# Decay attention with a mixture of experts: fixed key/query tiles with constant rows, decay rows on 64 partitions, weights in nine transfers

## The chip, the cores and the metric

The kernel runs on one NeuronCore of a Trainium2 chip, and the time is the device time of one execution in microseconds, as a median of several. A NeuronCore has a matrix engine (TensorE, in the profile PE, with its weight loads as PEld), a vector engine (VectorE, DVE), an activation engine (ScalarE, ACT), a general engine (GpSimd, POOL) and a queue engine (SyncE, SP), which issues the transfers (DMAs). Each engine works through its own instructions in order and waits on semaphores for the others.

## The reference

Eight batches of eight heads, 576 positions, head width 64. First a causal attention with decay, then a mixture of four experts, each with an attention of its own on the result, of which the gate takes two per row:

```python
scores = scale * q @ k.T                       # (8, 8, 576, 576)
cum = cumsum(log(clip(f, 1e-4, 1)))
attn = softmax(causal(scores + cum[i] - cum[j]))
x = concat_heads(attn @ v)                     # (8, 576, 512)
for e in range(4):                             # experts
    qe, ke, ve = x @ wq[e], x @ wk[e], x @ wv[e]
    ye = softmax(causal(scale * qe @ ke.T)) @ ve @ wo[e]
    out += gate_top2(x @ w_gate)[e] * ye
```

## The kernel before

**Pairs.** The unit of work is a pair: two heads of a batch ("a", 32 of them) or two experts ("m", 16). The first eight pairs, those of batches 0 and 1, are all attention; from then on four attention pairs and two expert pairs alternate. For a pair the kernel does these tasks, each a Python generator:

- `prep_attn` loads keys and queries (`kn`, `qn`, two transfers each), transposes them on PE (`tp`), copies the rounded part to the tile `kq` (ACT, L229), and the difference to `ka` (DVE, L230), eight of each per pair; two transfers copy `kq` rows to `ka`. `prep_moe` does the same with projections (`pp`).
- `max_pass` multiplies queries by keys (PE, L378, tile `m`) and takes the maximum of each row (DVE, L384, L395, L422, L428). The maxima are transposed, negated (ACT, L435, `ms`), and two transfers (L199, called in line 439) write them to row 68 of `kq`.
- `scores` makes two products for each block: L464 with `ka`, and L465 with `kq`, which carries the decay and the maximum. ACT takes the exponential (L481, L491, L496, L508), POOL sets the upper triangle to zero and adds up the rows (`R`).
- `attend` multiplies by the values (PE, L551, tiles `oa` and `ob`); `row_sums` and `apply_rows` divide; `moe_front` and `project_out` are the experts' gate, values and output.

**Decay.** `kq` holds 64 rows of keys and queries and five rows more: the product of the rows 64 to 68 adds decay, minus decay and minus the maximum. So the products take 68 and 69 rows (`K = 68`, `K = 69`). `decay_rows` works the decay out on 32 partitions (one pair of heads each, two halves of 576), then writes a table `ex` of 33 entries in DRAM, three transfers of ones and minus ones and two of the decay. `extra_rows` gives pair 0 and 1 (`DIRECT = 2`) their rows directly (two memsets on POOL, two transfers), and every later pair by one transfer of 5 rows from `ex`; an expert pair takes entry 32, whose decay is zero. The tiles `kq`, three of them, are taken in turn from a pool.

**Weights.** `load_weights` brings four matrices and the gate in 18 transfers through staging tiles; ACT rounds them (L175), POOL makes the remainder (L176).

**What sets the order.** Each task has a start and an end in units of pairs (`PLAN`, `HEAD`, `TAIL`, `W`), and a heap in the last lines of the function takes the generators' steps by their due time. So the tables write the order of the program; the tile framework then moves instructions on an engine a little by its own estimate. On the chip each engine keeps the order that results. `load_weights` is due from -1.0 to 0.2, that is before the first pair's scores.

## Time and profile before

| | |
|---|---|
| three runs, median (lowest, highest) | 796.29 us (794.36, 798.07) |
| the profiled execution | 794.9 us, of it the span 793.2 us |
| busy PE, PEld, DVE, ACT, POOL | 740.0, 600.7, 581.6, 472.8, 400.8 us |
| share of the span | 93%, 76%, 73%, 60%, 51% |
| moved by the DMA engines | 73.3 MB, 92 GB/s on average |

The span runs from the first to the last instruction of one execution. A busy share is an average over stages with different limits: a stage in which DVE or a transfer is waited for doesn't show in the 93% of PE. The rows below are therefore taken by stretch.

### The profile page before, as it was taken

The page shows a single profiled execution, that of the slowest core. Times are in us where ns is not written, and L with a number is a line of the kernel's source. Part 1 is how long each engine was busy: PE and PEld are TensorE (multiplying, and loading weights), DVE is VectorE, ACT ScalarE, POOL GpSimd, SP SyncE. Part 2 cuts the span into 40 slices and gives each one's busy share as a digit, 9 for nine tenths or more (in the row PEclk, how much of TensorE's full clock was granted, in tenths as well). Part 3 has the DMA queues.
Part 4 walks back from the last instruction along what each step waited for, and adds up shares of the span by engine and source line. Part 5 has one row for each costly group of instructions (what it writes and reads, how often), then busy time and mean ns, then how long its engine had stood idle before and what let it go on. Part 6 is the DMA issues. An engine that isn't in the chain of part 4 may idle for free.

```text
span 793.2 us, 16781 instructions
## 1 busy us (share of the span) xinstructions
PE 740.0 (93%) x5704; PEld 600.7 (76%) x5704; DVE 581.6 (73%) x1858; ACT 472.8 (60%) x1152; POOL 400.8 (51%) x763
## 2 busy tenths in 40 slices
PE   3698999998999999999999999999999999989987
PEld 2475678776897788877887778878887768869854
DVE  7557786898777797787777787778777877764633
ACT  5465664575657674676556665667655755555443
POOL 7556472556446564547444644465544564473270
PEclk9998999999999999999999999999999999999999
DMA  7865541254424632355323542256323442203103
GB/s 187 194 138 118 98 105 32 58 123 89 91 51 105 145 86 49 84 128 139 79 63 87 127 107 63 52 135 147 78 65 79 112 102 57 55 21 70 58 14 106
DMA packets 143231, 73.32 MB, mean 92 GB/s; under 512 B 124085, under 2 KB 124565, under 8 KB 143081
## 3 DMA queue, kind: packets, MB, share of 16 engines
q1 hardware_dynamic: 143147, 72.26, 39.9%
q8 instruction: 45, 0.74, 0.4%
q14 instruction: 39, 0.32, 0.1%
HBM read 32.68 MB, written 10.96 MB: 55 GB/s over the span
## 4 chain that ended last, share of the span: by engine, by line
PE 74%; DVE 8%; ACT 6%; DMA 5%; SPq 3%; issue 2%; POOL 2%; POOLq 0%; ACTq 0%; DVEq 0%
PE pp_m L352 13%; PE ob_a L551 9%; PE pv L276 6%; PE po L678 6%; PE s_a L464 6%; PE s_a L465 6%; PE m_a L378 5%; PE tp_a L221 3%; PE ob_m L551 3%; PE m_m L378 3%; PE s_m L464 3%; PE s_m L465 3%; PE oa_a L551 2%; DVE junk_a L384 2%; PE sm_a L594 2%
## 5 line engine op out<-in xcount | busy, mean ns | idle before, releaser
L230 DVE TENSOR_TENSOR ka_a<-tp_a,kq_a 64x288 fp32r<-64x288 f32 x256 | 113.0, 451 | 25.0 <-ACT kq_a L229 19.4
L384 DVE CUSTOM_DVE_ANT_0 junk_a<-m_a,mask 128x192 bf16<-128x192 f32 (+2 forms) x192 | 93.3, 486 | 48.2 <-PE m_a L378 28.6
L464 PE MATMUL s_a<-ka_a 128*128 128x320 f32 (+4 forms) x384 | 115.8, 319 | 1.7 <-ACT P_a L481 1.1
L378 PE MATMUL m_a<-kq_a 68*128 68x320 f32 (+4 forms) x384 | 103.5, 337 | 14.0 <-DMA kq_a<-chl 7.8
L229 ACT ACTIVATE kq_a<-tp_a 64x288 fp32r<-64x288 f32 x256 | 99.1, 403 | 28.7 <-DVE ka_a L230 18.8
L465 PE MATMUL s_a<-kq_a 69*128 69x320 f32 (+4 forms) x384 | 104.8, 302 | 3.1 <-DMA kq_a<-ms_a 3.1
L450 POOL TENSOR_SCALAR_AFFINE_SELECT P_a<-P_a 128x128 f32<-128x128 f32 x128 | 37.5, 295 | 107.5 <-ACT P_a L496 96.1
L483 POOL TENSOR_SCALAR_AFFINE_SELECT P_a<-P_a 128x256 f32<-128x256 f32 x64 | 26.1, 408 | 125.8 <-ACT P_a L481 124.1
L378 PEld LDWEIGHTS m_a<-kq_a 68*128 68x128 f32 (+1 forms) x384 | 65.5, 191 | 26.4 <-issue 9.1
L359 ACT ACTIVATE kq_m<-pp_m 64x288 fp32r<-64x288 f32 x128 | 51.5, 405 | 51.4 <-PE pp_m L352 29.9
L360 DVE TENSOR_TENSOR ka_m<-pp_m,kq_m 64x288 fp32r<-64x288 f32 x128 | 57.8, 454 | 31.6 <-ACT kq_m L359 27.0
L464 PEld LDWEIGHTS s_a<-ka_a 128*128 128x128 f32 (+1 forms) x384 | 71.1, 186 | 8.8 <-ACT P_a L496 2.2
L519 POOL TENSOR_TENSOR R_a<-P_a 128x448 f32<-128x448 f32 x64 | 73.2, 1144 | 4.1
L551 PE MATMUL ob_a<-P_a,va 128*64 128x320 f32 (+1 forms) x512 | 73.8, 433 | 0.9 <-ACT ms_m L435 0.4
L465 PEld LDWEIGHTS s_a<-kq_a 69*128 69x128 f32 (+1 forms) x384 | 70.1, 186 | 5.7 <-DMA kq_a<-ms_a 4.3
L551 PEld LDWEIGHTS ob_a<-P_a,va 128*64 128x64 f32 x512 | 36.0, 144 | 33.4 <-issue 8.0
L464 PE MATMUL s_m<-ka_m 128*128 128x192 f32 (+3 forms) x192 | 57.9, 316 | 1.9 <-ACT P_m L496 1.2
L384 DVE CUSTOM_DVE_ANT_0 junk_m<-m_m,mask 128x192 bf16<-128x192 f32 (+2 forms) x96 | 46.6, 485 | 17.7 <-PE m_m L378 14.1
L520 POOL TENSOR_TENSOR R_a<-R_a,P_a 128x320 f32<-128x320 f32 x64 | 55.9, 875 | 1.1
L465 PE MATMUL s_m<-kq_m 69*128 69x192 f32 (+2 forms) x192 | 52.5, 300 | 3.3 <-DMA kq_m<-ms_m 3.2
L378 PE MATMUL m_m<-kq_m 68*128 68x192 f32 (+2 forms) x192 | 48.0, 317 | 0.6 <-DVE mxt_m L395 0.3
L276 PE MATMUL pv<-vh,xh_a 128*128 128x260 f32 x160 | 47.1, 294 | 1.1 <-DVE ka_a L230 1.0
(189 smaller groups left out, 2071.8 us busy)
## 6 DMA issues: line engine op xcount, KB each, us to landing
ka_a<-kq_a SPq DMA_DIRECT2D x64, 288.0 KB
kn_a<-in_k_dram SPq DMA_DIRECT2D x64, 144.0 KB
qn_a<-in_q_dram SPq DMA_DIRECT2D x64, 144.0 KB
ka_m<-kq_m SPq DMA_DIRECT2D x32, 288.0 KB
va<-in_v_dram SPq DMA_DIRECT2D x64, 128.0 KB
out_dram<-outb SPq DMA_DIRECT2D x32, 256.0 KB
kq_a<-ex SPq DMA_DIRECT2D x30, 45.0 KB
kq_a<-ms_a SPq DMA_DIRECT2D x64, 2.5 KB
```

Of the source, the lines that this page charges most:

```text
L229: nc.scalar.activation(hv, src, AF.Copy)
L230: nc.vector.tensor_tensor(lo[:, h, gs], src, hv.bitcast(F32), ALU.subtract)
L276: nc.tensor.matmul(pv[:, :NV], l[c][:, t0 : t0 + 128], r[:, c], start=(n == 0), stop=(n == 3 * KC - 1))
L352: nc.tensor.matmul(pp[:, :HS], w[:, c, es], x[c][:, gs], start=(n == 0), stop=(n == 3 * KC - 1))
L360: nc.vector.tensor_tensor(lo[:, h, gs], src, hv.bitcast(F32), ALU.subtract)
L378: nc.tensor.matmul(dst, qB[0:K, h, i0 : i0 + dst.shape[0]], kB[0:K, h, j0:j1], start=True, stop=True)
L384: nc.vector.tensor_tensor_reduce(jk[:, :n], src, mask[:, MW - n :], 1.0, init, ALU.add, ALU.max, acc)
L464: nc.tensor.matmul(dst, kaf[:, c : c + m], qA[:, h, i0:i1], start=True, stop=False)
L465: nc.tensor.matmul(dst, kqf[0:K, c + h * S : c + h * S + m], qB[0:K, h, i0:i1], start=False, stop=True)
L519: g.tensor_tensor(r[:, h, 128:S], q[:, 320:768], q[:, 768:1216], ALU.add)
L520: g.tensor_tensor(r[:, h, 256:S], r[:, h, 256:S], q[:, 1216:1536], ALU.add)
L551: mm = nc.tensor.matmul(dst[64 * h : 64 * h + 64, c0 : c0 + rhs.shape[-1]], vs[h][0:kp, blk], rhs, start=first, stop=last,)
```

## The change

- Four fixed tiles `kq0` to `kq3` take turns. `constant_rows` fills the rows 64 to 127 once: ones on the key side, zeros on the query side, minus ones in two rows. So products take 128 rows (`K = 128`), and only the decay rows are brought for each pair.
- `decay_rows` works on 64 partitions, one head each, in one piece. The table `ex` has only the two decay rows per head: one transfer of them and one of zeros, in a task of its own. `extra_rows` brings them in two transfers per pair; only pair 0 takes them directly (`DIRECT = 1`, four transfers).
- The weights come in 9 transfers instead of 18, due from pair 1 to pair 4.
- The other constants move into a task (`constants`); the pool of `kn` and `qn` has four buffers instead of three; `chl` lies in another pool; a scratch area for DMAs is smaller.

```diff
-    nat = ctx.enter_context(tc.tile_pool(name="nat", bufs=3))
+    nat = ctx.enter_context(tc.tile_pool(name="nat", bufs=4))
...
+    kqs = [const.tile([128, 2, 2, S], F32R, name=f"kq{i}") for i in range(NKQ)]
...
+    def constant_rows(kq, eng):
+        eng.memset(kq[64:128, :, 0].bitcast(F32), 1.0)
+        nc.gpsimd.memset(kq[64:128, :, 1].bitcast(F32), 0.0)
+        nc.gpsimd.memset(kq[64:66, :, 1].bitcast(F32), -1.0)
+
+    constant_rows(kqs[0], nc.vector)
...
-    DIRECT = 2
-    ex = dram.tile([NX, 2, 5, 2, S], F32, name="ex")
+    DIRECT = 1
+    ex = dram.tile([NP + 1, 2, 2, S], F32, name="ex")
...
     def decay_rows():
...
-        for h in range(2):
-            hs = slice(h * S, (h + 1) * S)
-            nc.vector.tensor_tensor_scan(cum[:, hs], pos1[:NP], lf[:, hs], 0.0, ALU.mult, ALU.add)
-            nc.scalar.activation(chl[:NP, 0, h], cum[:, hs], AF.Copy, scale=INV_SCALE)
...
-        for kq, r0, r1, src in ((0, 2, 5, pos1), (1, 0, 2, neg1), (1, 4, 5, pos1)):
-            nc.sync.dma_start(
-                ex[:, kq, r0:r1].rearrange("x r h s -> x (r h) s"),
-                src.unsqueeze(1).to_broadcast([NX, 2 * (r1 - r0), S]),
-            )
-        nc.sync.dma_start(ex[:, 0, 0:2], chl.bitcast(F32))
-        nc.sync.dma_start(ex[:, 1, 2:4], chl.bitcast(F32))
-        yield 0.5
+        nc.vector.tensor_scalar(ft, ft, 1.0e-4, 1.0, ALU.max, ALU.min)
+        nc.scalar.activation(lf, ft, AF.Ln)
+        nc.vector.tensor_tensor_scan(cum, pos1, lf, 0.0, ALU.mult, ALU.add)
+        nc.scalar.activation(chl[:, 0], cum, AF.Copy, scale=INV_SCALE)
+        nc.vector.scalar_tensor_tensor(
+            chl[:, 1], cum, INV_SCALE, chl[:, 0].bitcast(F32), ALU.mult, ALU.subtract
+        )
+        yield 1.0
+
+    def spread_rows():
+        nc.sync.dma_start(ex[:NP].rearrange("x h r s -> (x h) r s"), chl.bitcast(F32))
+        nc.sync.dma_start(
+            ex[NP].rearrange("h r s -> (h r s)").rearrange("(p c) -> p c", p=128), zero
+        )
+        yield 1.0
...
+                for e in range(0, E, 2):
+                    parts.append(
+                        (w[e : e + 2].rearrange("e (c p) d -> p (e c) d", p=128), 2, slice(D * e, D * e + 2 * D))
                     )
...
     def extra_rows(kq, x):
         if x < DIRECT:
-            nc.gpsimd.memset(kq[64:69].bitcast(F32), 1.0)
-            nc.gpsimd.memset(kq[64:66, :, 1].bitcast(F32), -1.0)
-            nc.sync.dma_start(kq[64:66, :, 0].bitcast(F32), chl[x : x + 1].bitcast(F32))
-            nc.sync.dma_start(kq[66:68, :, 1].bitcast(F32), chl[x : x + 1].bitcast(F32))
+            for h in range(2):
+                src = chl[2 * x + h : 2 * x + h + 1].bitcast(F32)
+                nc.sync.dma_start(kq[64:66, h, 0].bitcast(F32), src)
+                nc.sync.dma_start(kq[66:68, h, 1].bitcast(F32), src)
             return
-        nc.sync.dma_start(
-            kq[64:69].bitcast(F32), ex[x].rearrange("k r h s -> r h k s")
-        )
+        src = ex[x].rearrange("h r s -> r h s")
+        nc.sync.dma_start(kq[64:66, :, 0].bitcast(F32), src)
+        nc.sync.dma_start(kq[66:68, :, 1].bitcast(F32), src)
...
-        kB, qB, K = u["kB"], u["qB"], 68
+        kB, qB, K = u["kB"], u["qB"], 128
...
-        qA, qB, K = u["qA"], u["qB"], 69
+        qA, qB, K = u["qA"], u["qB"], 128
...
-    W = dict(d1=-0.8, l0=-1.0, l1=0.2)
+W = dict(d1=-1.9, l0=1.0, l1=4.0, c0=-1.7, c1=-1.3, x0=-0.9)
...
-    task(-1.99, W["d1"], 1.0, decay_rows)
+    task(-1.999, W["d1"], 1.0, decay_rows)
+    task(W["c0"], W["c1"], 1.0, constants)
+    task(W["x0"], W["x0"], 1.0, spread_rows)
     task(W["l0"], W["l1"], 4.0, load_weights)
```

The tables `PLAN`, `HEAD` and `TAIL` are the same in both. How the order changes is seen best on SP. Before, these rows of SP end with the two transfers that bring pair 0's maxima to its `kq` (`st` are staged weights, `ka_a_1` is pair 1, `x2` means twice in a row):

```order
L169 DMA st_k_319<-in_moe_wk_dram 128x4x64 x2
L199 DMA ka_a_1_254<-kq_a_1_255 64x2x576
L169 DMA st_k_333<-in_moe_wk_dram 128x4x64 x2
L169 DMA st_q_340<-in_moe_wq_dram 128x4x64 x2
L169 DMA st_q_353<-in_moe_wq_dram 128x4x64 x2
L199 DMA ka_a_1_254<-kq_a_1_255 64x2x576
L191 DMA kq_a_1_255<-chl 2x2x576
L192 DMA kq_a_1_255<-chl 2x2x576
L164 DMA st_o_365<-in_moe_wo_dram 128x512
L211 DMA kn_a_2_389<-in_k_dram 96x6x64 x2
L211 DMA qn_a_2_390<-in_q_dram 96x6x64 x2
L199 DMA kq_a_0_163<-ms_a_0_305 1x5x128 x2
```

Now the same place reads so (`kq_111`, `kq_112`, `kq_113` are the tiles of pairs 0, 1, 2):

```order
L244 DMA kn_a_3_476<-in_k_dram 96x6x64 x2
L244 DMA qn_a_3_477<-in_q_dram 96x6x64 x2
L282 DMA va_104<-in_v_dram 128x4x64
L231 DMA ka_a_2_345<-kq_113 64x2x576
L282 DMA va_104<-in_v_dram 128x4x64
L287 DMA va_104<-in_v_dram 64x2x64
L202 DMA st_v_504<-in_moe_wv_dram 128x8x64
L282 DMA va_105<-in_v_dram 128x4x64
L231 DMA ka_a_2_345<-kq_113 64x2x576
L282 DMA va_105<-in_v_dram 128x4x64
L287 DMA va_105<-in_v_dram 64x2x64
L231 DMA kq_111<-ms_a_0_295 1x5x128 x2
```

All weights but the first part have gone behind pair 0's maxima; keys and queries of pairs 2 and 3 and the values of pairs 0 and 1 have come ahead of them. On ACT the exponentials of pair 0 (`P_a_0`) now stand among the weights:

```order
L472 ACTIVATE ms_a_0_295<-mp_a_0_293 10x128
L205 ACTIVATE vh<-st_v_504 128x4x128
L521 ACT_TABLE_LOAD
L521 ACTIVATE P_a_0_327<-s_a_0_329 128x512
L205 ACTIVATE vh<-st_v_584 128x4x128
L205 ACTIVATE vh<-st_v_637 128x4x4
L521 ACTIVATE P_a_0_327<-s_a_0_377 128x512
L205 ACTIVATE kh<-st_k_698 128x4x128
L531 ACTIVATE P_a_0_327<-s_a_0_409 128x2x256
L472 ACTIVATE ms_a_1_417<-mp_a_1_415 10x128
L205 ACTIVATE kh<-st_k_766 128x4x128
```

Before, all eight conversions of weights (`vh`, `kh`, `qh`, `oh`, two each) stood ahead of the first exponential. On DVE, the difference for pair 2 (`ka_a_2`) stood among the maxima of pair 1, and now stands among those of pair 0 (`junk_a_0`):

```order
L263 TENSOR_TENSOR ka_a_2_345<-tp_a_2_352,kq_113 64x288
L126 CAST sel_100<-self_180 128x128
L421 ISA junk_a_0_253,mxs_a_0_233<-m_a_0_248,mask,mxt_a_0_235 128x256
L421 ISA mxs_a_0_233 128x1
L263 TENSOR_TENSOR ka_a_2_345<-tp_a_2_397,kq_113 64x288
L263 TENSOR_TENSOR ka_a_2_345<-tp_a_2_352,kq_113 64x288
L421 ISA junk_a_0_257,mxs_a_0_233<-m_a_0_255,mask 128x448
```

So DVE has a third pair's differences to make before the maxima of pair 0 are complete.

## Rows read from the trace of the kernel before

**Rows 1.** The page: span, and granted TensorE clock in 40 slices (tenths).

```profile
span 793.2 us, 16781 instructions
...
PEclk9998999999999999999999999999999999999999
```

**Rows 2.** Windows: busy us (count) per engine, granted clock, DMA share, GB/s.

```profile
0.00:20.00 20.00, 6.21 (x28) 4.63 (x28) 14.10 (x27) 10.37 (x22) 14.45 (x37) 1.00 0.77 186
20.00:39.40 19.40, 12.01 (x41) 8.84 (x40) 10.41 (x38) 8.06 (x14) 10.24 (x9) 1.00 0.88 195
39.40:50.00 10.60, 9.93 (x44) 8.07 (x46) 5.65 (x18) 8.00 (x22) 6.65 (x13) 1.00 0.77 164
50.00:110.00 60.00, 54.40 (x381) 38.48 (x382) 46.38 (x142) 34.89 (x88) 32.97 (x64) 0.91 0.52 108
...
200.00:700.00 500.00, 488.54 (x3925) 405.37 (x3923) 387.53 (x1269) 313.00 (x772) 254.36 (x489) 1.00 0.40 90
```

**Rows 3.** The chain that ended last, 0 to 40 us: start, length, what.

```profile
0.81 2.68 DMA fl<-in_f_dram
...
7.37 4.91 DMA kn_a<-in_k_dram
...
33.71 3.45 DMA st_o<-in_moe_wo_dram
```

**Rows 4.** Timeline, 18 to 45 us: start, length, engine, line, in brackets idle before.

```profile
18.93 1.30 PE L378 MATMUL m_a<-kq_a 68*128 68x192 f32 x4 [3.04 <-DMA kq_a<-chl]
...
31.19 1.30 PE L378 MATMUL m_a<-kq_a 68*128 68x192 f32 x4 [4.72 <-DMA kq_a<-chl]
...
32.06 1.55 SPq L199 DMA_DIRECT2D kq_a<-ms_a  x2
...
35.53 0.51 PE L465 MATMUL s_a<-kq_a 69*128 69x192 f32 x1
...
39.42 1.08 ACT L481 ACTIVATE P_a<-s_a 128x512 f32<-128x512 f32 x2
...
44.15 0.08 DVE L384 DVE_READ_ACCUMULATOR2_ANT mxs_a<- 128x1 f32 x1
```

**Rows 5.** Timeline, DVE: eight differences' rate, first and last of pair 0's maxima.

```profile
13.08 2.87 DVE L230 TENSOR_TENSOR ka_a<-tp_a,kq_a 64x288 fp32r<-64x288 f32 x6 [0.47 <-ACT kq_a L229]
...
19.78 0.36 DVE L384 CUSTOM_DVE_ANT_0 junk_a<-m_a,mask 128x192 bf16<-128x192 f32 x1 [2.04 <-PE m_a L378]
...
25.66 0.28 DVE L428 TENSOR_REDUCE mxs_a<-mx_a 64x2 f32<-64x128 f32 x1
```

**Rows 6.** Timeline, decay rows on DVE (two halves each), and a memset on POOL.

```profile
3.52 1.03 DVE L126 TENSOR_SCALAR fl<-fl 32x576 f32<-32x576 f32 x2 [1.38 <-DMA fl<-in_f_dram]
...
4.79 2.67 DVE L130 TENSOR_TENSOR_SCAN cum<-one,fl 32x576 f32<-32x576 f32 x2 [0.24 <-ACT fl L127]
...
8.37 2.01 POOL L189 MEMSET kq_a<- 5x2304 f32 x1
```

**Rows 7.** Transfers issued in the first 33 us: count, KB each.

```profile
ex<-chl SPq DMA_DIRECT2D x2, 297.0 KB
...
ex<-one SPq DMA_DIRECT2D x1, 445.5 KB
```

**Rows 8.** Groups by form: busy us, mean ns of one.

```profile
L378 PE MATMUL m_a<-kq_a 68*128 68x320 f32 x128 | 45.5, 357 | 0.9 <-ACT kq_a L229 0.9
...
L464 PE MATMUL s_a<-ka_a 128*128 128x320 f32 x128 | 44.3, 347 | 0.3 <-ACT P_a L496 0.2
```

**Rows 9.** Timeline, PE: the same 16 matmuls of pair 0 and of pair 1.

```profile
49.88 3.44 PE L551 MATMUL ob_a<-P_a,va 128*64 128x320 f32 x16
...
62.24 2.16 PE L551 MATMUL ob_a<-P_a,va 128*64 128x320 f32 x16
```

**Rows 10.** Timeline and SP's waits: one transfer from the decay table; SP's longest wait.

```profile
35.35 0.78 SPq L194 DMA_DIRECT2D kq_a<-ex  x1
...
SPq L199 <- ACT kq_m L359: 95.3, 24, 10.2
```

More of the change, by code (lines that the diff above doesn't have):

```diff
@@ L92, in tile_decay_attention_moe @@
     v_moe = const.tile([128, 5, E, D], F32, name="vm")
-    for t in v_att + [v_moe]:
-        nc.gpsimd.memset(t[64:128, 4], 0.0)
     NPL = 3
-    p_last = []
-    for i in range(NPL):
-        t = const.tile([128, 2, 64], F32, name=f"pl{i}")
-        nc.gpsimd.memset(t[64:128], 0.0)
-        p_last.append(t)
-    n_last = [0]
+    p_last = [const.tile([128, 2, 64], F32, name=f"pl{i}") for i in range(NPL)]
+    n_last = [0]
+    p_user = [None] * NPL
+    NKQ = 4
+    kqs = [const.tile([128, 2, 2, S], F32R, name=f"kq{i}") for i in range(NKQ)]
@@ new lines, in tile_decay_attention_moe, with constants @@
+    constant_rows(kqs[0], nc.vector)
+    def constants():
+        nc.gpsimd.memset(mask, 0.0)
+        nc.gpsimd.affine_select(
+            mask[:, MW - 128 :], mask[:, MW - 128 :], [[-1, 128]], ALU.is_ge, NEG, base=0, channel_multiplier=1
+        )
+        yield 0.2
+        constant_rows(kqs[1], nc.gpsimd)
+        yield 0.2
+        for t in v_att + [v_moe]:
+            nc.gpsimd.memset(t[64:128, 4], 0.0)
+        for t in p_last:
+            nc.gpsimd.memset(t[64:128], 0.0)
+        nc.gpsimd.memset(ones_col, 1.0)
+        yield 0.1
+        for p in range(2):
+            sf = work.tile([128, 128], F32, tag="mx0", name=f"self{p}")
+            nc.gpsimd.memset(sf, 0.0)
+            for h in range(2):
+                blk = sf[:, 64 * h : 64 * h + 64]
+                base = 32 * (2 * p + h)
+                for r in range(2):
+                    nc.gpsimd.affine_select(
+                        blk, blk, [[0, 64]], ALU.not_equal, 1.0, base=-(base + r), channel_multiplier=1
+                    )
+            nc.vector.tensor_copy(sel[p], sf)
+            yield 0.1
+            constant_rows(kqs[2 + p], nc.gpsimd)
+            yield 0.1
+        for t, sg in ((up, 1), (low, -1)):
+            nc.gpsimd.memset(t, 1.0)
+            nc.gpsimd.affine_select(
+                t, t, [[-sg, E], [sg, E]], ALU.is_gt, 0.0, base=0, channel_multiplier=0
+            )
+        yield 0.1
@@ L106, in tile_decay_attention_moe @@
     NP = B * NPH
-    NX = NP + 1
-    DIRECT = 2
-    ex = dram.tile([NX, 2, 5, 2, S], F32, name="ex")
+    DIRECT = 1
+    ex = dram.tile([NP + 1, 2, 2, S], F32, name="ex")
+    NR = B * H
     fl = prob.tile([128, 2, 1536], F32, tag="P", name="fl")
-    ft, lf = (fl[:NP, i, : 2 * S] for i in range(2))
-    nc.sync.dma_start(ft, f.rearrange("b (p h) s -> (b p) (h s)", h=2))
-    chl = pair.tile([128, 2, 2, S], F32R, tag="kq", name="chl")[:NX]
-    nc.gpsimd.memset(chl[NP:].bitcast(F32), 0.0)
@@ new lines, in tile_decay_attention_moe @@
+    ft, lf = (fl[:NR, i, :S] for i in range(2))
+    nc.sync.dma_start(ft, f.rearrange("b h s -> (b h) s"))
+    chl = rows.tile([128, 2, S], F32R, tag="R", name="chl")[:NR]
+    pos1 = rows.tile([128, 2, S], F32, tag="R", name="one")[:NR, 0]
+    nc.vector.memset(pos1, 1.0)
+    zero = const.tile([128, 4 * S // 128], F32, name="zero")
+    nc.vector.memset(zero, 0.0)
+    def decay_rows():
+        cum = prob.tile([128, 2, 1536], F32, tag="P", name="cum")[:NR, 0, :S]
+        nc.scalar.activation(lf[:, 0:1], pos1[:, 0:1], AF.Ln)
+        nc.vector.tensor_scalar(ft, ft, 1.0e-4, 1.0, ALU.max, ALU.min)
[4 more added lines that the diff above has]
+            chl[:, 1], cum, INV_SCALE, chl[:, 0].bitcast(F32), ALU.mult, ALU.subtract
+        )
+        yield 1.0
@@ L261, in moe_front @@
             vm = [v_att[0], v_att[1]]
+            assert all(u is None or u.get("attended") for u in v_user[:2]) and natt[0] == B * NPH
         else:
```

131 lines of the change are left out of this document (53 added, 78 removed).

## The prediction

> **What bounds the kernel now.** I read the windows first. From 200 to 700 us PE is busy for 488.5 of 500 us: there every engine but PE waits, and a change that leaves PE's work as it is can only shift that stretch [rows 2]. The head is different. In the first 39.4 us PE has 18.2 us of work and DVE 24.5; the DMA engines are busy for 0.77 and 0.88 of the time and move 186 and 195 GB/s [rows 2]. So the head waits for transfers, and the chain of waits agrees: it begins with the input f, goes on through a transfer of keys that took 4.91 us, and comes to a weight transfer of 3.45 us just ahead of the first exponential [rows 3]. The timeline gives the places: PE waited twice for decay rows (the first maxima start at 18.93 us, pair 1's at 31.19), SP issued pair 0's maxima at 32.06, the first product with them ran at 35.53, the first exponential at 39.42 [rows 4].
>
> Then comes a ramp. From 50 to 110 us PE is busy 54.4 of 60 us and DVE 46.4 [rows 2], in pairs that are all attention. PE's time there is inflated: the same 16 matmuls took 3.44 us at 49.88 and 2.16 at 62.24 [rows 9], so at 49.88 TensorE worked at its lower level, though the page shows 9 in those slices [rows 1]: the row of clocks doesn't show the time ahead of its first event. Between 50 and 110 us the mean is 0.91, so it fell again for a while [rows 2]. At full clock PE would have spare time there, and DVE with 77% is near to setting the pace.
>
> So what the change is worth is read in the first 45 us: how much earlier DVE and ACT come through the same work. Later work stands in nearly the same order, and the gain is carried to the end.
>
> **Part by part.**
>
> *Rows 128 instead of 68 and 69.* A matmul of 68 rows and 320 columns took 357 ns on average, one of 128 rows and 320 columns 347 [rows 8]. Rows cost PE nothing; I take 0, with a possible gain that is a rival below.
>
> *Decay on 64 partitions.* DVE needed 1.03 us for two clips and 2.67 for two scans, each on 576 columns [rows 6]. One of each is left: about 1.9 us less on DVE. A memset of 64 rows and 1,152 columns is new on DVE, ahead of f's arrival at 3.49 us (0.81 + 2.68) [rows 3], while DVE waits 1.38 us for it [rows 6]: nothing, and about 1 us if f came at once. From f's arrival the chain is clip 0.5, logarithm, scan 1.3, copy and difference; with two thirds of a microsecond for each of the three others, an estimate from the 0.5 and 1.3 about them, DVE is through at 7.5 us.
>
> *Bytes ahead of pair 0's maxima.* SP had issued 12 transfers of keys and queries, three of ones (445.5, 297 and 148.5 KB), two of decay (594), four copies to `ka`, f, and 12 weight transfers of 128 KB and one of 256, before it came to `ms` at 32.06 [rows 4, 7]. By the shapes in the order a transfer of keys has 144 KB (96 x 6 x 64 x 4 bytes), a copy 288 and f 144: with small ones 6,345 KB in all. In the new order stand ahead of it f (144), 16 of keys and queries (2,304), one of decay (288), six copies to `ka` (1,728), values of pairs 0 and 1 (576), one weight part (256), some 60 of small ones: 5,359 KB. At the same rate that is 32.06 x 5,359 / 6,345 = 27.1 us. Issue (1.55 us) and landing (35.53 - 33.61 = 1.9) as before [rows 4] put the first product with maxima at 30.6, and the first exponential about 1.1 us later, the time of its four products at the low clock: 31.7 instead of 39.42. That is **7.7 us earlier**. The 2.8 us (36.6 to 39.42) that ACT spent on a weight and a table load after the products were ready are gone if the one weight ahead of them is there, which was issued nine rows earlier.
>
> *Work on DVE ahead of the ramp.* Before, DVE is through with the maxima of pairs 0 and 1 and the differences of pairs 0, 1 and 2 at 44.2 us [rows 4]. One pair's maxima take 6.16 us (19.78 to 25.94), and eight differences 8 x 0.48 = 3.83 [rows 5]. So the same work is 2 x 6.16 + 3 x 3.83 = 23.8 us. From 7.5 us on without a gap it is done at 31.3; the keys of pair 1 no longer stand behind 891 KB of ones, and the decay rows of pair 0, ready at 7.5 and issued by SP within some 2 us, are in place at about 11.5 us if they land 1.9 us later, as the maxima did; DVE gets to the maxima no earlier, with pair 0's differences done at 11.3. With no gap is not to be had: ACT's copies and PE at the low clock feed DVE in turns. I allow 2 to 4 us, 34.3 at the middle: **9.9 us earlier**, with bounds of 12.9 (no gap) and 7 (6 us of gaps, a quarter of the work, as in the ramp where DVE idles 13.6 of 60 us [rows 2]).
>
> *Constants.* POOL fills 64 rows of four tiles, in 11 memsets of 1,152 elements a row (a twelfth is DVE's): by the 2.01 us for 2,304 elements [rows 6] about 1 us each, 11 us, where five memsets fall away in turn. POOL has 5.55 us free in the first 20 us and 9.2 in the next 19.4, when it loses the weights' remainders [rows 2]. Pair 0's tile and the mask come first; I take 0, and 2 us if the table's transfers for pair 2 have to wait for the last rows, inside the bounds of DVE's gaps.
>
> *Weights.* 2 MB go from the head to pairs 1 to 4. From 50 to 110 us the DMA engines are busy 0.52 of the time [rows 2]; that hides them. Their rounding moves too: nine pieces on ACT and POOL, which are busy 35 and 33 of 60 us there. I take 0, and up to 9 as a rival.
>
> *Two transfers per pair instead of one.* One from the table cost 0.78 us on SP [rows 10]; 47 more are 37 us over the whole run. SP spends 95.3 us in one kind of wait alone [rows 10], so they lie in its idle time: 0, and at most the 0.78 us for each of the first pairs, where SP is full; that stands in the 27.1 above. The page "DMA: Bandwidth & Descriptors" of the Trainium skill, in its rules for kernel authors, speaks against this part: many small transfers should be made one large one, since under 64 KB one pays mostly overhead. By that rule the split of 45 KB into two of 9 KB would waste most of the saved bytes, and this part would be a loss of the issue time and no gain; no row here shows that the path waits for it.
>
> *Four tiles, four buffers.* With three tiles the table's transfer for pair 4 waited for pair 1's scores; now for pair 0's. It can only release SP earlier; I count 0.
>
> **The sum.** Two paths meet in the ramp, ACT's with 7.7 and DVE's with 9.9. The later one decides at first, DVE in the end; I take 9.0, between them. The profiled execution took 794.9 us (span 793.2 and 1.7 around it), so 785.9; the three runs have their median 1.4 above it. I predict **786**.
>
> **The rivals.**
>
> *The clock rises earlier.* Pair 0's scores ran at the low clock until the first long row of `ob` matmuls [rows 9]. Products with 128 rows do more in the array; if the clock rises in pair 0's scores, and the fall between 50 and 110 us stays away, PE saves up to 3.44 - 2.16 = 1.28 of each 3.44 us: of 10 us of scores 3.7, and of the later fall (0.09 of 60 us, 5.4 us) about as much. DVE near its bound takes back part: 4 to 8 more, 778 to 782. For it: PE was busy 9.93 of 10.6 us from 39.4 on at the low clock [rows 2], with products of few rows. Against: no row shows that rows matter. 0.2.
>
> *The weights stall ACT.* Four conversions now stand among pair 0's exponentials, and ACT can't pass them; each waits for a transfer issued after the maxima. If each makes ACT wait 2.25 us, the 9 us are spent. A weight took 3.45 us to land [rows 3]. For it: SP issues them one after the other. Against: they run in parallel, so the first wait covers most of the next. Result 790 to 797: 0.23.
>
> *Slower: the low clock lasts.* In the new order DVE feeds PE with more gaps, and if TensorE stayed at the low level through pairs 0 to 3, PE would lose 37% of its time (1.28 of 3.44 [rows 9]) while it is the one waited for. The gain of 9 is gone after 24 us more of it, that is if the clock rose at about 67 us instead of some 43; at 80 us the kernel would take 800. Against: `ob` of pair 0 still stands as 20 matmuls in a row, and with such a row the clock rose. 0.07.
>
> **How the numbers follow.** My forecast has 0.5 (782.5 to 789 by the bounds of DVE's gaps), the others 0.2, 0.23 and 0.07. A change under 0.5%, 4 us, can't be told from none, so faster means under 792.3. That takes all of the first two and half of the third: 0.81; within 0.5% the other half: 0.12; slower 0.07. The range runs from 775 (no gap on DVE and the early clock: 794.9 - 12.9 - 7) to 794 (most of the third rival).
>
> **What would show it.** Right: the first maxima on PE near 12 us, pair 0's `ms` transfers issued near 27, the first exponential near 32, pair 1's maxima through at 34, and the rest shifted by the same amount; DVE's idle time in the first 50 us (19.8 now) some 8 to 10 less. Early clock: `ob` of pair 0 near 2.2 us for its 16 matmuls. Weights: ACT idle behind `st` transfers among L521 to L548. The prediction would be wrong if SP came to `ms` as late as before because it waits for copies of pair 2, or if the shift at 45 us were lost again in pairs 2 to 7.

## The result, and the profile after

The changed kernel takes **786.4 us** (median of 4 runs, 786.28 to 788.18). The kernel before took 795.3 in the same comparison (792.63 to 798.07). The ratio is 0.9891, with a 95% interval from 0.9852 to 0.993. The prediction was 786. The profiled execution took 786.41, its span is 784.7 us against 793.2 [rows 1]. The page of the changed kernel, its span, the busy time of each engine and the row of granted clocks:

```profile
span 784.7 us, 16842 instructions
...
PE 733.1 (93%) x5704; PEld 593.9 (76%) x5704; DVE 582.5 (74%) x1856; ACT 469.4 (60%) x1151; POOL 404.8 (52%) x770
...
PEclk9999999999999999999999999999999999999999
```

PE has the same 5,704 matmuls as before, where its line on the page was `PE 740.0 (93%) x5704`. A span is PE's busy time and its idle time: 740.0 + 53.2 before, 733.1 + 51.6 now. So of the 8.5 us won, 6.9 stand in PE's busy time, on the same matmuls, and only 1.6 in its waits, while the prediction priced waits. Over the whole span this hides where each was won. Cut at the last exponential of pair 0 and at that of pair 6, first before, then after:

```profile
0.00:47.48 47.48, 25.63 (x99) 19.75 (x101) 28.41 (x77) 23.94 (x50) 28.89 (x55) 1.00 0.84 191
47.48:138.56 91.08, 85.43 (x622) 65.96 (x620) 67.32 (x208) 52.57 (x133) 47.64 (x92) 0.94 0.43 90
138.56:793.20 654.64, 628.91 (x4987) 514.96 (x4983) 485.84 (x1575) 396.26 (x972) 324.31 (x618) 1.00 0.37 86
...
0.00:41.47 41.47, 25.23 (x103) 20.35 (x103) 27.49 (x82) 20.63 (x48) 23.80 (x56) 1.00 0.96 174
41.47:131.51 90.04, 82.42 (x614) 63.43 (x615) 69.35 (x200) 55.15 (x134) 55.62 (x97) 0.96 0.47 103
131.51:784.70 653.19, 625.48 (x4991) 510.10 (x4986) 485.70 (x1577) 393.63 (x972) 325.39 (x619) 1.00 0.35 83
```

Up to pair 0 PE waits 5.6 us less and works 0.4 less; that is what the prediction priced. From there to pair 6 it works 3.0 us less and waits 2.0 more. Behind pair 6 it again works 3.4 less and waits 2.0 more, and there the granted clock reads 1.00 in both, so half of the 6.9 us is not the clock's.

The same windows as [rows 2] (busy us and count of PE, PEld, DVE, ACT, POOL; granted clock, DMA share, GB/s):

```profile
0.00:20.00 20.00, 9.12 (x43) 7.41 (x43) 15.08 (x37) 9.91 (x23) 16.80 (x43) 1.00 0.91 167
20.00:39.40 19.40, 14.04 (x52) 11.03 (x50) 10.85 (x39) 9.44 (x22) 4.93 (x9) 1.00 0.99 183
39.40:50.00 10.60, 10.25 (x73) 7.70 (x73) 8.25 (x28) 7.59 (x20) 10.55 (x17) 1.00 0.89 168
50.00:110.00 60.00, 52.73 (x379) 38.68 (x379) 50.58 (x138) 38.72 (x93) 38.61 (x69) 0.94 0.52 115
...
200.00:700.00 500.00, 486.51 (x3932) 400.27 (x3931) 385.59 (x1265) 308.61 (x762) 256.88 (x493) 1.00 0.37 87
```

In the third line PE is as busy as before (10.25 and 9.93 us) and gets through 73 matmuls in place of 44. The row of clocks says 1.00 in both.

The timeline of the changed kernel at the places of [rows 4] and [rows 6] (start, length, engine, line; idle time before it in brackets):

```profile
3.94 0.47 DVE L155 TENSOR_SCALAR fl<-fl 64x576 f32<-64x576 f32 x1 [1.09 <-DMA fl<-in_f_dram]
...
7.32 0.75 DVE L159 SCALAR_TENSOR_TENSOR chl<-cum,chl 64x576 fp32r<-64x576 f32 x1 [0.75 <-ACT chl L158]
...
11.54 0.82 PE L415 MATMUL m_a<-kq 128*128 128x192 f32 x2
...
29.59 1.64 SPq L231 DMA_DIRECT2D kq<-ms_a  x2
...
32.58 0.51 PE L502 MATMUL s_a<-kq 128*128 128x192 f32 x1
...
33.76 1.28 ACT L521 ACT_TABLE_LOAD   x1 [3.64 <-PE s_a L502]
...
35.05 0.60 ACT L521 ACTIVATE P_a<-s_a 128x512 f32<-128x512 f32 x1
...
35.14 0.08 DVE L421 DVE_READ_ACCUMULATOR2_ANT mxs_a<- 128x1 f32 x1
...
45.24 2.16 PE L583 MATMUL ob_a<-P_a,va 128*64 128x320 f32 x16
```

The decay rows are ready at 8.07. The first maxima run at 11.54 (18.93 before), pair 1's maxima are through at 35.2 (44.2 before), the first exponential runs at 35.05 (39.42 before). The last line is the row of matmuls of [rows 9]: 2.16 us at 45.24, where before it took 3.44 at 49.88. So TensorE was at its upper level here already. The weight loads of the same shape show when it rose:

```profile
39.69 0.33 PEld L502 LDWEIGHTS s_a<-kq 128*128 128x128 f32 x1
...
40.23 0.33 PEld L502 LDWEIGHTS s_a<-kq 128*128 128x128 f32 x1
...
40.90 0.19 PEld L415 LDWEIGHTS m_a<-kq 128*128 128x128 f32 x1
41.01 0.19 PEld L501 LDWEIGHTS s_a<-ka_a 128*128 128x128 f32 x1
```

A load of 128 x 128 took 0.33 us until 40.4 and 0.19 from 40.9 on, in the midst of pair 0's scores. Before, the rise came within the `ob` row, after 49.88.

How the lead grew is read from the last exponential of a pair (the one into `pl`): pair 0 at 41.47 against 47.48 before, 6.0 us ahead; pair 3 10.9 ahead, pair 5 only 4.9, pair 6 7.1, the end 8.5. So the shift was not carried to the end as it was. Something takes and gives in the ramp. Between 64 and 75 us the windows show it:

```profile
64.00:66.00 2.00, 2.00 (x17) 1.47 (x13) 2.00 (x2) 1.59 (x4) 2.00 (x4) 1.00 0.64 150
66.00:68.00 2.00, 0.22 (x2) 0.14 (x1) 1.97 (x4) 0.06 (x1) 1.36 (x3) 0.99 0.03 6
68.00:71.40 3.40, 3.40 (x13) 1.56 (x15) 3.00 (x8) 1.93 (x4) 0.82 (x2) 0.50 0.24 52
71.40:74.80 3.40, 3.40 (x30) 3.12 (x27) 1.81 (x7) 1.99 (x4) 0.70 (x2) 1.00 0.82 204
```

PE has work for 0.22 of 2 us, and then TensorE runs at half clock for 3.4 us: 13 matmuls there, 30 in the next 3.4. A second such stretch came from 88.4 on, behind six microseconds (82 to 88) in which PE was busy for 3.9. The kernel before had 6.8 us at the low level from 73 on and 3.4 from 90.

### The profile page after: what moved, and what is told of

It reads as the page before. It is cut to its first block, busy times and chain, and to the rows that moved or that the text cites. A ratio compares the mean times of both kernels' runs of the same rounds, so it can differ in the third digit from the quotient of the medians.

```text
span 784.7 us, 16842 instructions
## 1 busy us (share of the span) xinstructions
PE 733.1 (93%) x5704; PEld 593.9 (76%) x5704; DVE 582.5 (74%) x1856; ACT 469.4 (60%) x1151; POOL 404.8 (52%) x770
## 4 chain that ended last, share of the span: by engine, by line
PE 74%; DVE 10%; ACT 6%; DMA 6%; issue 2%; SPq 1%; POOL 1%; POOLq 0%; DVEq 0%; ACTq 0%
PE pp_m L389 13%; PE ob_a L583 8%; PE pv L313 7%; PE po L710 7%; PE s_a L501 6%; PE m_a L415 6%; PE s_a L502 5%; PE tp_a L254 4%; PE s_m L502 3%; DMA kq<-ms_m 3%; PE s_m L501 3%; PE m_m L415 3%; PE sm_a L626 2%; DVE ka_a L263 2%; DMA kq<-ms_a 2%
## 5 line engine op out<-in xcount | busy, mean ns | idle before, releaser
L263 DVE TENSOR_TENSOR ka_a<-tp_a,kq 64x288 fp32r<-64x288 f32 x256 | 113.0, 450 | 19.7 <-ACT kq L262 9.7
L262 ACT ACTIVATE kq<-tp_a 64x288 fp32r<-64x288 f32 x256 | 99.9, 402 | 36.0 <-DVE ka_a L263 19.9
L415 PE MATMUL m_a<-kq 128*128 128x320 f32 (+4 forms) x384 | 104.4, 334 | 5.0 <-DVE mxs_a L421 2.9
L502 PE MATMUL s_a<-kq 128*128 128x320 f32 (+4 forms) x384 | 101.4, 299 | 2.1 <-DMA kq<-ms_a 2.1
L397 DVE TENSOR_TENSOR ka_m<-pp_m,kq 64x288 fp32r<-64x288 f32 x128 | 58.1, 454 | 45.1 <-ACT kq L396 43.1
L396 ACT ACTIVATE kq<-pp_m 64x288 fp32r<-64x288 f32 x128 | 51.8, 404 | 62.4 <-PE pp_m L389 40.3
L487 POOL TENSOR_SCALAR_AFFINE_SELECT P_a<-P_a 128x128 f32<-128x128 f32 x128 | 37.6, 298 | 88.1 <-ACT P_a L536 85.6
L415 PEld LDWEIGHTS m_a<-kq 128*128 128x128 f32 (+1 forms) x384 | 65.7, 190 | 17.5 <-DVE mxs_a L421 7.8
L502 PEld LDWEIGHTS s_a<-kq 128*128 128x128 f32 (+1 forms) x384 | 69.3, 185 | 4.7 <-DMA kq<-ms_a 3.3
L502 PE MATMUL s_m<-kq 128*128 128x192 f32 (+2 forms) x192 | 50.4, 297 | 3.3 <-DMA kq<-ms_m 3.2
L415 PE MATMUL m_m<-kq 128*128 128x192 f32 (+2 forms) x192 | 48.4, 318 | 1.5 <-DVE mxt_m L432 0.7
```

The costliest lines, as they stand in the source:

```text
L262: nc.scalar.activation(hv, src, AF.Copy)
L263: nc.vector.tensor_tensor(lo[:, h, gs], src, hv.bitcast(F32), ALU.subtract)
L397: nc.vector.tensor_tensor(lo[:, h, gs], src, hv.bitcast(F32), ALU.subtract)
L415: nc.tensor.matmul(dst, qB[0:K, h, i0 : i0 + dst.shape[0]], kB[0:K, h, j0:j1], start=True, stop=True)
L487: return nc.gpsimd.affine_select(pv, pv, [[1, 128]], ALU.is_ge, 0.0, base=0, channel_multiplier=-1)
L502: nc.tensor.matmul(dst, kqf[0:K, c + h * S : c + h * S + m], qB[0:K, h, i0:i1], start=False, stop=True)
```

## The experiments

All times are medians, and each ratio is to runs of the kernel before on the same chip.

**The row count alone, taken back.**

```diff
-        kB, qB, K = u["kB"], u["qB"], 128
+        kB, qB, K = u["kB"], u["qB"], 68
...
-        qA, qB, K = u["qA"], u["qB"], 128
+        qA, qB, K = u["qA"], u["qB"], 69
```

> The changed kernel with the row count of the products alone set back (68 rows in the maxima, 69 in the scores). Theory A, the order of the transfers and the work ahead of the ramp make the gain, the row count is free: the same head to within 0.3 us (first exponential at 35.0, pair 1's maxima through at 35.2), the same level of TensorE's clock in pair 0's scores, and 786 to 787.5. Rival B, products of 128 rows raised the clock earlier and that is a part of the gain: the head up to 40 us is the same, but the matmuls of pair 0's scores stay at the low level (0.33 us a weight load) until the row of matmuls into ob at about 45, that row starts at the low level (3 us and more for 16 matmuls in place of 2.16), and the kernel takes 788 to 791.

790.5 us, ratio 0.9927 (0.99 to 0.9955). The first exponential comes at 35.80. The `ob` row of pair 0 in its timeline:

```profile
46.26 4.11 PE L583 MATMUL ob_a<-P_a,va 128*64 128x320 f32 x16
```

All of it is at the low level, as B said, and there are 13.7 us at half clock from 88.5 on and 6.8 more from 163.6 on. But fewer rows also changed the order of the instructions in the ramp, so this run alone doesn't price the rows.

**96 rows.** The same two lines with 96. Here each engine's instructions stand in the order of the changed kernel, so that only the rows differ.

> The changed kernel with products of 96 rows in place of 128. Theory A, the rise of the clock answers to the share of rows in a graded way: it comes between 40.7 us (128 rows) and the end of ob at about 50 (68 rows), the median is 787 to 789.5. Rival B, all or nothing: either as with 128 rows (rise at 40 to 42, 786 to 787) or as with 68 (ob's row at 3.4 us or more, 789.5 to 791.5).

792.7 us, ratio 0.9954 (0.9929 to 0.9979). Neither theory held: the clock rose as early as with 128 rows (0.33 to 0.19 us at 39.8; `ob` in 2.16 us), and the kernel is as slow as with 68. The windows of the same place show why:

```profile
66.00:68.00 2.00, 0.25 (x1) 0.25 (x1) 2.00 (x6) 0.00 (x0) 0.99 (x3) 0.78 0.00 0
68.00:71.40 3.40, 3.40 (x12) 1.57 (x14) 3.24 (x9) 1.94 (x4) 0.83 (x2) 0.50 0.13 30
71.40:74.80 3.40, 3.40 (x21) 2.69 (x18) 0.51 (x3) 1.03 (x2) 0.00 (x0) 0.63 0.92 221
```

After the same idle stretch the low level lasts 6.8 us (67.1 to 73.9) in place of 3.4, and 6.8 again from 87.6 on. Of the 4.0 us by which this span is longer, 2.5 stand ahead of pair 6's last exponential and 1.5 behind it, where neither trace has a fall ahead of its last 2 us. One trace is one execution, but all runs agree: the mean granted clock of the twelve with 96 rows is 0.983 to 0.993, that of the four of the changed kernel 0.993 to 0.996. By the averages (0.9888 and 0.9950) that is some 10 us more at half clock in a run, an estimate of up to 5 us, and 5 were measured.

**The weights early again.**

```diff
-W = dict(d1=-1.9, l0=1.0, l1=4.0, c0=-1.7, c1=-1.3, x0=-0.9)
+W = dict(d1=-1.9, l0=-1.0, l1=0.2, c0=-1.7, c1=-1.3, x0=-0.9)
```

> The changed kernel with its nine weight transfers moved back to the head (eight of them ahead of pair 0's maxima, 2.1 MB in place of 0.26). Theory A, bytes ahead of the maxima's transfers set the time: 6,741 KB in place of 5,488, so these transfers are issued at 29.6 x 6,741 / 5,488 = 36.4 us, the first exponential comes 6 to 7 us later than 35.0, and the kernel takes 791 to 794. Rival B, DVE's and PE's work for pairs 0 to 2 sets the time and the bytes lie beside it: issue at 29 to 31 us, 786 to 788.

787.8 us, ratio 0.9901 (0.9878 to 0.9924). The head is what A said, if a little less: `ms` is issued at 34.56, the first exponential comes at 40.98, pair 0's last at 45.99, 4.5 us late. At pair 5 none of that is left (109.48 against 109.72); at pair 6 it is 2.0 us late, with one more fall of 3.4 us on the way. The end is B's.

**The bytes of the ones again.** Three transfers into a place that nobody reads.

```diff
+        for r0, r1 in ((0, 3), (3, 5), (5, 6)):
+            nc.sync.dma_start(spare[:, r0:r1], pos1.unsqueeze(1).to_broadcast([NR, r1 - r0, S]))
```

> The changed kernel with three further transfers of ones from the chip to memory (864 KB, as many bytes as the kernel before had for its table of ones, but read by nobody), behind the decay rows. Theory A, the bytes alone delay the head: 864 KB at 185 GB/s are 4.7 us; pair 1's keys and the first maxima come 2 to 4.7 us later, and the kernel takes 788.5 to 791. Rival B, these bytes lie beside other work: the head moves by under 1 us, 786 to 787.5.

784.3 us, ratio 0.9853 (0.9825 to 0.988), against 0.9891 of the change itself. `ms` is issued at 29.62 (29.59 in the changed kernel). The first maxima come 1.6 us later (13.09), pair 0's last exponential 1.4. So the bytes cost the head a third of what A's rate says; SP's queue moved a copy to `ka` and the values of pair 1 (576 KB) behind `ms` in their place. At the end nothing of it is seen, and the time is below both ranges. In the ramp this kernel has one stretch at the low level in place of two.

**The kernel before, with its weights late.**

```diff
-    W = dict(d1=-0.8, l0=-1.0, l1=0.2)
+    W = dict(d1=-0.8, l0=1.0, l1=4.0)
```

> The kernel before, with its weight transfers planned over pairs 1 to 4 and nothing else changed. Theory A, the weights' place is the main part of the change: pair 1's maxima are through by 40 in place of 44.2 us, the first exponential comes before 36, and the kernel takes 789 to 791. Rival B, the table of decay rows with its ones and its place ahead of the keys decides, and the weights only filled time in which DVE and PE waited for pair 1's rows (its maxima begin at 31.2): the head stays within 1 us, 794 to 796.

797.8 us, ratio 1.0026 (1.0003 to 1.0049): the part alone gains nothing. `ms` is issued later than before (35.68), since pair 3's keys and the values move up into the free place in SP's queue. A fell, and B's head and time too. Yet pair 6's last exponential comes 5.6 us earlier than before (132.94). It is lost behind it: this trace has 13.6 us at the low level there (from 163.0, 610.1 and 712.5 on), the kernel before has none, and the rest takes 661.6 us in place of 654.6. Over its twelve runs the mean granted clock is 0.984 to 0.994; the kernel before had 0.989 to 0.998 beside it.

**The kernel before, with 128 rows.** Four fixed tiles, filled once (with zeros); `chl` lies in another pool and the scratch area is smaller, as in the changed kernel.

```diff
+    kqs = [const.tile([128, 2, 2, S], F32R, name=f"kq{i}") for i in range(4)]
+    nc.vector.memset(kqs[0][64:128].bitcast(F32), 0.0)
+    for t in kqs[1:]:
+        nc.gpsimd.memset(t[64:128].bitcast(F32), 0.0)
...
-        kq = pair.tile([128, 2, 2, S], F32R, tag="kq", name="kq" + nm)
+        kq = kqs[n_pair[0] % 4]
...
-        kB, qB, K = u["kB"], u["qB"], 68
+        kB, qB, K = u["kB"], u["qB"], 128
...
-        qA, qB, K = u["qA"], u["qB"], 69
+        qA, qB, K = u["qA"], u["qB"], 128
```

> The kernel before with the row count alone: four fixed key/query tiles whose rows 64 to 127 are filled with zeros once, and products of 128 rows; the decay table of 33 partitions with its ones and the early weights stay. Theory A, 128 rows let TensorE's clock rise in pair 0's scores: weight loads of 0.14 to 0.19 us in place of 0.33 before the row of matmuls into ob, that row 2.16 us in place of 3.44, PE's busy time 734 to 737 in place of 740.0, and 790 to 793 us. Rival B, the clock rose earlier in the changed kernel because of its order, not its rows: ob at 3.4 us as before, 794.5 to 797.

808.9 us, ratio 1.014 (1.0106 to 1.0174). From its timeline, two lines:

```profile
25.84 1.30 PE L384 MATMUL m_a<-kq 128*128 128x192 f32 x4 [5.24 <-DMA kq<-chl]
...
52.69 2.16 PE L557 MATMUL ob_a<-P_a,va 128*64 128x320 f32 x16
```

The second is A's sign: the clock rose in pair 0's scores, ahead of `ob`, and PE's busy time is 736.4. The first shows a cost of the new order: PE waits for the decay rows of pair 0 until 6.9 us later than before, since seven weight transfers stand ahead of them on SP, where one did. But that is not where the time went. Pair 0 and pair 6 end only 1.8 us later than before; 8.0 of the 9.9 us stand behind pair 6 (662.7 and 654.6), where PE works as long (628.9) and waits 8.1 us more. The edit made the order anew up to the end, so as a price of the rows it is of no use.

**The decay rows late.**

```diff
+        for _ in range(5):
+            nc.vector.tensor_tensor_scan(spare, pos1, ft, 0.0, ALU.mult, ALU.add)
```

> The changed kernel with five more scans (some 6.7 us of DVE, results unused) ahead of the decay rows' scan, so that the first maxima come at some 18 us, as in the kernel before (18.93), in place of 11.5; rows, weights and transfers stay as changed. Theory A, as predicted, DVE's path through the maxima and differences of pairs 0 to 2 decides: pair 1's maxima are through at 40 to 42 in place of 35.2, and the kernel takes 791 to 794. Rival B, DVE's waits in the head and the ramp take the delay up: under 2 us of it is left at the end, 786 to 788.5. PE's busy time stays at 733 within 1.5 if no further fall of the clock comes with it.

785.6 us, ratio 0.9846 (0.9817 to 0.9875). The first maxima come at 17.50, 6 us late. Pair 0's last exponential is 3.3 late, pair 3's 0.4 ahead. A fell; the end is B's, a little under its range. The tenth attention pair's last exponential comes at 200.13, against 199.72 in the changed kernel and 206.44 before.

**All three head parts back, 128 rows kept.** The edits of the three runs on the weights, the ones and the decay rows, together.

> The changed kernel with three of its parts taken back together, while the products keep 128 rows: the weights early, 864 KB of ones for a table that nobody reads, and five unused scans that hold the decay rows back. Each of them alone cost 1.4 us or less. Theory A, as predicted, the head decides, and one part back was covered by the others: pair 1's maxima are through at 41 or later, pair 0's last exponential comes at 47 or later (47.48 in the kernel before), and the kernel takes 791 to 796. Rival B, the ramp from 50 to 115 us takes up what the head loses, and the gain is that of the clock: 785 to 789.

785.4 us, ratio 0.987 (0.9842 to 0.9897). Pair 0's last exponential comes at 45.61, pair 3's at 78.38 (87.24 before), pair 5's at 109.44, the tenth attention pair's at 200.14 (199.72 in the changed kernel, 206.44 before). The time and the ramp are B's. Its six runs have mean clocks of 0.996 to 0.998, against 0.993 to 0.996, by the averages 3.6 us less at half clock or up to 1.8 us of time (an estimate), and its ratio is 0.2% better: with that set aside, giving back 4.1 of the 6.0 us at pair 0 cost nothing that can be seen.

**The table of exponentials early.** One more row on ACT, else the changed kernel's order.

```diff
             chl[:, 1], cum, INV_SCALE, chl[:, 0].bitcast(F32), ALU.mult, ALU.subtract
         )
+        nc.scalar.activation(lf[:, 0:1], pos1[:, 0:1], AF.Exp)
```

> The changed kernel with one exponential of one column right behind the decay chain, so that ScalarE's table for exponentials is loaded there and not between pair 0's first product and its first exponential; every other row stands where it stood. Theory A, the way over the first exponential decides the time: 1.28 us less there, 785.0 +- 0.5. Rival B, it doesn't decide: the first exponential comes at 33.8 in place of 35.05, and at the end nothing is seen of it, 786 to 787.

787.5 us, ratio 0.9896 (0.9868 to 0.9924). Both missed a step. The load of 1.28 us now stands at 8.30 ahead of ACT's copies of pair 0:

```profile
8.30 1.28 ACT L162 ACT_TABLE_LOAD   x1
9.60 0.20 ACT L162 ACTIVATE fl<-one 64x1 f32<-64x1 f32 x1
9.70 2.16 ACT L263 ACTIVATE kq<-tp_a 64x288 fp32r<-64x288 f32 x6
...
35.49 0.60 ACT L522 ACTIVATE P_a<-s_a 128x512 f32<-128x512 f32 x1 [3.74 <-PE s_a L503]
```

It makes the first maxima 1.9 us later (13.44) and the first exponential not earlier. Pair 0 ends 1.2 us late, the span is 1.7 us longer. That doesn't show a delay of the head coming through: at pair 6 only 0.2 us is left of it (with 3.4 us less at the low level on the way), the other 1.5 arise behind, where this trace has a fall of 3.4 us from 162.9 on, and the medians can't tell the two kernels apart (0.9896 and 0.9891).

**The maxima products of pairs 0 and 1 made twice.**

```diff
+            for _ in range(2 if nm in ("_a0_0", "_a0_1") else 1):
                 nc.tensor.matmul(
```

> The changed kernel with every product of the maxima of pairs 0 and 1 made twice into the same place (36 matmuls more, some 14 us of PE at the low level, where PE is idle for 16.2 of the first 40.7 us). Theory A, the clock rises by how much PE has done with all rows: it rises some microseconds earlier than 40.7, the first weight loads of 0.14 to 0.19 us come before 36, and in spite of the added work the kernel takes 784 to 787. Rival B, the rise does not answer to it: PE becomes the one waited for in the head, the first exponential comes 3 us or more later, and the kernel takes 788 to 793.

779.6 us, ratio 0.9779 (0.9751 to 0.9807), the fastest of all: 24 matmuls more (not 36), whose results are overwritten by the same values, and 1.1% off the changed kernel. The clock rose by 37.6, less early than A said. The windows of its ramp, from 45 and from 50 us on, are:

```profile
45.00:115.00 70.00, 65.65 (x517) 50.56 (x518) 56.83 (x174) 46.51 (x114) 47.52 (x84) 1.00 0.55 121
...
50.00:110.00 60.00, 55.70 (x429) 42.92 (x431) 49.54 (x151) 42.30 (x104) 42.52 (x79) 1.00 0.57 125
```

There is no fall of the clock in the ramp, and from 50 to 110 us 429 matmuls stand where the changed kernel has 379. But the order of the ramp changed with it, and most of the gain is not the clock's. PE is busy for 735.3 us, 2.2 more than in the changed kernel, and idle for 44.8, 6.8 less. Between pair 0 and pair 6 this span is 6.3 us shorter, 3.6 of it in PE's busy time and 2.8 in its waits. A fall of 3.4 us comes late, at 743.5. And its four runs have mean clocks of 0.991 to 0.999, by the average (0.9960 against 0.9950) 1.6 us less at half clock than the changed kernel; the fastest of them, 778.83 us, has the lowest.

**The same with the kernel before**, 68 and 69 rows.

> The kernel before, with 68 and 69 rows as it has them, and every product of the maxima of pairs 0 and 1 made twice into the same place. Theory A, more work on TensorE in the head lets the clock rise earlier, with few rows too: pair 0's row of matmuls into ob takes under 3 us in place of 3.44, the stretches at the low level between 50 and 115 us (10.2 us before) become shorter, and the kernel takes 788 to 793. Rival B, it takes products of 128 rows, or the gain of the doubled products in the changed kernel came from another order in the ramp: 794 to 799.

793.5 us, ratio 0.9968 (0.9941 to 0.9995). In the profiled run pair 0's `ob` row is at the low level (4.11 us at 53.89), against A, and no fall follows, as A said. This execution was the fastest of twelve, though; the mean clocks of the twelve go down to 0.987, so in others the clock fell. The median lies between the two ranges. PE's idle time is 48.0 us against 53.2 before. The window of the ramp:

```profile
58.00:115.00 57.00, 54.38 (x427) 42.17 (x424) 49.05 (x150) 39.98 (x99) 37.21 (x71) 1.00 0.59 123
```

**Doubled maxima and the early table together.**

> The changed kernel with the doubled maxima products of pairs 0 and 1 (779.6 us in an earlier run) and the table for exponentials loaded early, in the same order of instructions otherwise. Theory A, the table load on the way costs its 1.28 us: 778 to 779. Rival B, it costs nothing: 779 to 781.

782.2 us, ratio 0.9837 (0.9803 to 0.9872): no gain, as in the run on the table alone, and above both ranges.

**The 14 profiled runs side by side.** *Low* is the time at the low level between the last exponentials of pair 0 and pair 6: twice what the granted clock lacks to 1.00, summed over windows of 1 us. The rise in the head is not in it: in the four kernels with 68 rows the clock rose only 5.0 to 8.5 us behind pair 0's last exponential, and the row of clocks reads full until then. *Behind* is the same from pair 6 on, without the last 4 us. The clock is the average over all runs of a kernel, not the profiled one alone (the kernel before has three values, one for each of three comparisons).

| kernel | rows | pair 0 | pair 6 | low | behind | span | clock |
|---|---|---|---|---|---|---|---|
| before | 68 | 47.48 | 138.56 | 10.2 | 0 | 793.2 | 0.9930 to 0.9945 |
| before, weights late | 68 | 49.28 | 132.94 | 3.4 | 13.6 | 794.6 | 0.9888 |
| before, maxima twice | 68 | 50.05 | 134.73 | 0 | 0 | 789.0 | 0.9952 |
| before, 128 rows | 128 | 49.25 | 140.38 | 10.2 | 0 | 803.1 | 0.9877 |
| changed | 128 | 41.47 | 131.51 | 6.8 | 0 | 784.7 | 0.9950 |
| 68 rows | 68 | 42.47 | 136.37 | 13.7 | 6.8 | 790.1 | 0.9888 |
| 96 rows | 96 | 41.03 | 134.02 | 13.6 | 0 | 788.7 | 0.9888 |
| weights early | 128 | 45.99 | 133.51 | 10.2 | 3.4 | 787.1 | 0.9938 |
| ones back | 128 | 42.88 | 128.48 | 3.4 | 0 | 782.1 | 0.9970 |
| table early | 128 | 42.69 | 131.72 | 3.4 | 3.4 | 786.4 | 0.9940 |
| decay late | 128 | 44.77 | 133.06 | 6.8 | 0 | 784.2 | 0.9955 |
| head back | 128 | 45.61 | 132.88 | 6.8 | 0 | 783.7 | 0.9973 |
| maxima twice | 128 | 42.96 | 126.66 | 0 | 3.4 | 780.1 | 0.9960 |
| twice, table early | 128 | 41.67 | 127.21 | 3.4 | 3.4 | 780.2 | 0.9905 |

A straight-line fit through the 14 gives pair 6 = 90.9 + 0.85 x pair 0 + 0.64 x low, with standard errors of 0.14 and 0.10. It is an estimate over kernels of different order (the points lie 1.6 us about it). The term of the low level holds up; that of the head does not: through the ten versions of the changed kernel alone the fit gives 0.42 x pair 0, with a standard error of 0.28, and 0.62 x low, with 0.10. The 0.85 comes from setting the kernels before against the changed ones, which differ in more than the head.

## Why the prediction was right, and where its reasons were not

*The size.* The number was right by luck. The forecast had 9.0, all from the head and carried to the end. The head came out 6.0 us ahead at pair 0, but the runs that give 3.3 and 4.1 us of that back (decay late, head back) end no later, and their tenth attention pair ends 0.4 us behind the changed kernel's, where that one leads the kernel before by 6.7. So the head's share of the gain is small. The rows, costed at nothing, are worth some 5 us in the new order. These two errors met. What makes up the rest isn't shown: the lead at pair 6 is 7.05 us, the shorter time at half clock gives some 0.64 x 3.4 = 2.2 of it by the fit, the head by the two fits anything from 2.5 to 5.1 (by the tenth attention pair, less), and 1.5 more come behind pair 6. There PE's busy time fell by 3.4 at full clock; as the kernel before with 128 rows has the same 628.9 us there as with 68, the rows alone don't explain that.

*Products of 128 rows, "0 with a rival".* This is a step that failed. With the order left alone, 96 rows in place of 128 bring the ratio from 0.9891 to 0.9954 (the intervals just touch at 0.993; and from 0.9896 in the run on the table, whose interval ends below the one of 96 rows): 0.6% or some 5 us. One product costs the same (between 200 and 700 us one of 320 columns took 342 ns with 68 rows, 337 with 128); it is the time at the low level that differs, in the windows of both kernels and in the mean clocks of all their runs. That is the price of the rows in the new order. Rows alone don't set the clock: the kernel before has 68 and the averages 0.9930 to 0.9945, near the changed kernel's 0.9950. The rival "the clock rises earlier" named the mechanism but put 4 to 8 us on top of the forecast, and named the rise as the sign. The rise is early with 96 rows too; the fall decides.

*Bytes ahead of pair 0's maxima, 7.7 us.* Mis-sized, and for a wrong cause. `ms` was issued at 29.59 (27.1 forecast) and the first exponential came at 35.05 (31.7): 2.5 from the issue, and 1.4 since the table load of 1.28 us, taken as gone, still stands behind the first products; the way from issue to product was 0.5 shorter. In proportion to the bytes ahead of it, `ms` would have gone out at 31.2 with the ones back (5,783 to 5,488 of the expectation's KB, which have 1,000 bytes; the prediction's 5,359 are the same bytes) and at 36.4 with the weights early. It went out at 29.62 and 34.56: the bytes push it, by less than their share. The Trainium skill's rule on small transfers (page "DMA: Bandwidth & Descriptors", rules for kernel authors), which the prediction weighed, got no test: no run joins the two small transfers again.

*DVE's path, 9.9 us.* Right in itself: pair 1's maxima through at 35.2 (34.3 forecast), the chain of the decay rows at 8.07 (7.5). The sign that was to go with it was wrong: DVE's idle time in the first 50 us fell from 19.8 to 15.8, by 4.0 and not 8 to 10. DVE did the rest of the gain as more work in the same time.

*"The gain is carried to the end."* This step failed too. 3 to 4.5 us of a late head are gone by pair 5 (weights early, decay late, head back); 1.4 to 2.0 stand again at pair 6, and 0.4 or nothing at the tenth attention pair. All three edits also make the order of the ramp anew. The one run that leaves the order alone (early table) is 1.2 us late at pair 0 and 0.2 at pair 6, with less time at half clock, so it settles nothing.

*The weights: 0, with 9 as a rival.* Right: the rival's sign, ACT idle behind `st` transfers, is 1.51 us ahead of the scores, nothing among pair 0's exponentials, 0.2 at 43.4 and 1.71 at 81.4. Early weights give a ratio of 0.9901 against 0.9891, which can't be told from none. Alone, in the kernel before, the part gains nothing.

*The slower rival* would have needed the low level until 67 us; it ended at 40.9.

*Open.* Why a late head costs nothing, that is what sets the pace of the ramp, was not found; DVE's busy time there rose from 46.4 to 50.6 of 60 us, PE's fell. The kernel with the head back and the one with late decay rows make up 2.1 to 2.4 us behind pair 6 (650.8 and 651.1 us from there to the end, the changed kernel 653.2), which is not explained. Decay on 64 partitions, the constants on POOL, and the split transfers were not tried alone. Nor was a kernel with the changed order and 68 rows, since fewer rows made another order.

## What to carry to other kernels

Set span = PE's busy time + its idle time for both kernels before looking at waits, and do it stage by stage: over the whole span a gain in the head's waits and a loss in the ramp's cancel, and less busy time on the same matmuls can, but need not, be the clock. A row of granted clocks that reads full ahead of its first event hides a low level; the length of one repeated weight load doesn't. Compare the granted clocks of all runs and not of one trace, since the falls differ from one execution to the next. Useless matmuls, with the order that they made, were worth 1.1% here, most of it not by the clock: so try another order of the ramp. And before a shift of the head is counted to the end, delay the head and see; use an edit that leaves the order alone, or the reordering will be what you measure.
